# Output projection of a decode step: the last row group of wo cut into four pieces, its last row in two halves

## The chip, the cores and the metric

One core of one Trainium2 chip runs the whole kernel. The metric is device time in microseconds (us), the median of several executions. Engines are named as in the profile: PE is TensorE (PEld its weight loads), DVE is VectorE, ACT is ScalarE, POOL is GpSimd, SP is SyncE, whose queue issues all transfers here.

## What is computed

A decode step for two batch rows of width 640: cached attention with 32 heads over 4096 positions, a SiLU feed-forward, and a sigmoid gate that mixes the two.

```python
q = (x @ wq).reshape(B, 1, 32, 128)                    # x: (2, 1, 640)
p = softmax(einsum("bhqd,bhkd->bhqk", q, k_cache) * 128 ** -0.5)
o = einsum("bhqk,bhkd->bhqd", p, v_cache)              # caches: (2, 32, 4096, 128) f32
a = o.reshape(B, 1, 4096) @ wo                         # wo: (4096, 640)
b = silu(x @ w1) @ w2                                  # w1: (640, 1728)
g = sigmoid((x * gate_w).sum(-1, keepdims=True))
out = g * a + (1 - g) * b                              # (2, 1, 640)
```

All is float32. The change touches only `o @ wo`, its sum with the feed-forward's part, and the way out to memory.

## The kernel before

The kernel streams 298 MB from memory once. Sixteen items (8 groups of four heads, times 2 batch rows) each load a slab of keys and one of values, 8 MB each; POOL and DVE form the scores, ACT the exponentials, PE the weighted values. Three slabs of the on-chip memory ("v", "b", "a") are refilled in turn; slabs "v" and "b" take wo at the end, when the keys and values that lay in them are used up.

All transfers go through the SP queue in the order of the text. wo is 4096 x 640, seen as 32 "rows": one row is 128 partitions x 640 columns, 320 KB. Eight rows make a group (PR = 8), four groups make wo (NP = 4). `load_wo` (L284 to L298) issues groups 0 and 1 as one transfer, group 2 as two halves, and group 3, into slab "b", as three pieces: rows 0 to 4 (FIRST = 5), rows 5 and 6, and row 7. Each piece has its own semaphore.

PE multiplies wo by the gated attention output `oP` (each row is a contraction over 128 partitions; `oP` is the stationary operand, wo streams). Two forms are used. `in_halves` (L547) handles a row of 640 columns as two halves of 320 columns on two strips of 32 PSUM partitions, into the PSUM bank `early` (ps_acc), and does so for groups 0 to 2; the feed-forward's output was added into the same bank at the start of the kernel. `in_quarters` (L580) handles a row as four quarters of 160 columns on four strips, into the bank `acc` (ps_0), for the eight rows of group 3. Between the two `merge` (L567) brings `early` over into `acc`: ACT copies 128 x 320 from PSUM to on-chip memory (`partial`), and four matmuls with the 0/1 matrix `join` add the right strips together and set `acc`. Each matmul call of float32 stands as two MATMUL records in the trace. At the end DVE copies `acc` (128 x 160) into `ot` (L891), and SP sends eight rows of 160 floats to the output (L892).

`Flow.op` records each operation with the names that it reads and writes. A wait is made for the last writer of a name that is read; for PSUM names there is one more rule (L45, L46): an operation that reads a PSUM bank also waits for every other engine's operation that read the bank since it was last written. `once` and `spans` (L914) put stretches of an engine's program into a loop that runs once; the numbers there count operations.

Of the kernel before, what the change touches and what calls it, by code (L numbers as in the profile page):

```python
# [5 lines left out]
ALU = mybir.AluOpType  # L6
# [152 lines left out]
def gated_decode(nc, x, kc, vc, wq, wo, w1, w2, gate, out):  # L159
    P = 128  # L160
# [17 lines left out]
    G = 4  # L178
    W = D // G
    W2 = D // 2  # L180
    NP = HQ // 2
    PR = 2 * Q
    FIRST = 5
    LEAD = HB // 2
    PACED = (NP - 2) * PR
    items = [(hq, b) for hq in range(HQ) for b in range(B)]
# [7 lines left out]
    def sb(name, shape, align=32):  # L194
        return nc.alloc_sbuf_tensor(name, shape, F32, align_bytes=align)[tuple([slice(None)] * len(shape))]
# [9 lines left out]
    def part(n, *ks):  # L205
        return [f"{n}.{k}" for k in (ks or range(8))]
# [18 lines left out]
    he = sb("he", [P, FR, B])  # L225
    seq = sb("seq", [P, 2 * FR, HB])
    join = sb("join", [P, 2, HB + 1])
    turned = sb("turned", [P, FR * 32])
    mask = sb("mask", [P, B])
    spaced = sb("spaced", [P, FR, 32])  # L230
# [13 lines left out]

    ps_q, ps_o, ps_v, ps_acc, ps_t, ps_m, ps_0, ps_1 = (bank(f"ps{i}") for i in range(8))
    oT = ps_m[:64, 256:512].rearrange("p (n r) -> p n r", r=32)
    early, acc = ps_acc[:, :W2], ps_0[:, :W]

    h_q, h_e, h_v, h_o = (f.sem(n) for n in ("next_q", "weights", "values", "rows"))

# [4 lines left out]
    PD = PR * D  # L255


    partial = slab["v"][:, (NP - 1) * PD :][:, :W2]
    ot = slab["v"][:, (NP - 1) * PD + W2 :][:, :W]

    def kslab(i):
        return "a" if i % 2 == 0 else "b"
# [21 lines left out]
    def load_wo(g):  # L284

        n, at = ("v", g * PD) if g < NP - 1 else ("b", 0)
        if g == 0:
            src = wo[: 2 * PR * P, :].rearrange("(g p n) d -> p g (n d)", g=2, n=PR)
            to = slab["v"][:, : 2 * PD].rearrange("p (g c) -> p g c", g=2)
            f.dma("SP", to, src, writes=part("v", 0, 1), after=v_users)  # L290
            return
        if g == 1:
            return
        src = wo[g * PR * P : (g + 1) * PR * P, :].rearrange("(p n) d -> p (n d)", n=PR)
        cuts = (0, PD // 2, PD) if g < NP - 1 else (0, FIRST * D, PD - D, PD)
        after = f.users(part(n)) if g == NP - 1 else v_users
        for k, (c0, c1) in enumerate(zip(cuts, cuts[1:])):
            f.dma("SP", slab[n][:, at + c0 : at + c1], src[:, c0:c1], writes=part(n, g % (NP - 1) + k), after=after)  # L298
# [25 lines left out]
    f.op("POOL", lambda: G_.memset(pz, 0.0), writes=["pz"])  # L324
    f.op("POOL", lambda: G_.memset(seq, 0.0), writes=["seq"])

    out_rows = out.rearrange("b s (n d) -> (s n) b d", n=G)
    f.dma("SP", out_rows, oP[0:P:HB, :W], reads=["oP"], writes=["out"])

    f.op("DVE", lambda: V.memset(ones, 1.0), writes=["ones"])  # L330
    f.op(
# [79 lines left out]
            )  # L411

    H_AT = FH * HD
    X_AT = H_AT + B * F
# [127 lines left out]
    def heads(g):  # L544
        return [f"oP{g}{u}{b}" for u in range(2) for b in range(B)]

    def in_halves(g):  # L547

        for k in range(PR):
            s_ = g * PR + k  # L550

            def fn(k=k, s_=s_):
                to = 64 * (s_ % 2) if s_ < PACED else 0
                for n in range(2):
                    at = 32 * s_ + LEAD // 2 * n
                    last = T_.matmul(  # L556
                        early[to + 32 * n : to + 32 * n + 32, :],
                        oP[:, at : at + 32],
                        slab["v"][:, s_ * D + n * W2 : s_ * D + (n + 1) * W2],
                        start=(s_ == 0),  # L560
                        stop=(s_ in (PACED - 1, PACED + PR - 1)),
                    )
                return last

            f.op("PE", fn, reads=part("v", g + (g == NP - 2 and k >= PR // 2)) + heads(g), writes=["ps_acc"])

    def merge():  # L567
        f.op("ACT", lambda: S_.copy(partial, early), reads=["ps_acc"], writes=["partial"])

        def fn():  # L570
            for n in range(G):
                e, c = divmod(n * W, W2)
                last = T_.matmul(
                    acc[32 * n : 32 * n + HB + 1, :], join[:, e, :], partial[:, c : c + W], start=True, stop=False
                )
            return last

        f.op("PE", fn, reads=["partial", "join"], writes=["ps_0"])

    def in_quarters(g):  # L580
        for k in range(PR):
            at = LEAD + 32 * (g * PR + k)

            def fn(k=k, at=at):
                for n in range(G):
                    last = T_.matmul(  # L586
                        acc[32 * n : 32 * n + HB + 1, :],
                        oP[:, at : at + HB + 1],
                        slab["b"][:, k * D + n * W : k * D + (n + 1) * W],
                        start=False,  # L590
                        stop=(k == PR - 1),
                    )
                return last

            f.op("PE", fn, reads=part("b", (k >= FIRST) + (k == PR - 1)) + heads(g), writes=["ps_0"])

    ffn_out("v")

# [254 lines left out]
    for i in range(N + 1):  # L853
# [30 lines left out]
        if i + 1 < N:  # L884
            query(i + 1, by=[ops["relay", i]], loop=i)
            copy_q(i + 1)
    for g_ in range(NP - 1):
        in_halves(g_)
    merge()
    in_quarters(NP - 1)  # L890
    f.op("DVE", lambda: V.tensor_copy(ot, acc), reads=["ps_0"], writes=["ot"])  # L891
    f.dma("SP", out_rows, ot[0:P:HB, :], reads=["ot"], writes=["out"], signal=s_out)  # L892


    def land():
# [15 lines left out]
    f.plan()  # L911
    for e in ("SP", "POOL"):
        f.run(e)
    spans = {"ACT": (14, 34), "DVE": (100, 220), "PE": (len(f.ops["PE"]) - NP * PR - 1, len(f.ops["PE"]))}  # L914
    for e, (a, b) in spans.items():
        ops, at = f.ops[e], 0
        while at < len(ops):
# [35 lines left out]
```

## Time and profile before

| | us |
|---|---|
| median of 3 runs | 695.7 (695.59 to 695.74) |
| span of the profiled execution, first to last instruction | 694.2 |
| time outside that span (median less span) | 1.5 |
| transfer queue's share of 16 engines' span | 99.4% |
| last matmul of wo to the end of the span | about 2.1 |

The profile is of one execution. Its page has the span, the busy time of each engine, the transfer queues, the chain of work that ended last and the costliest groups of instructions. The trace behind it answers further questions: the chain in order of time, the timeline of a stretch, the groups by shape, the waits, and busy time and the granted PE clock by stretch. A row of the timeline gives start, length, engine, line, operation, operands and count of a merged run of instructions, and in brackets the idle time of that engine before it with what ended it. Ends of matmuls are modelled. In rows by shape, "busy, mean ns" gives the total in us and the mean of one in ns.

### The profile page before, as it was taken

What the parts mean: (1) busy time and instruction counts of PE and PEld (TensorE: products, weight loads), DVE (VectorE), ACT (ScalarE), POOL (GpSimd) and SP (SyncE); (2) the same over time, 40 slices, a digit from 0 to 9 for tenths busy, and PEclk for the clock granted to TensorE, in tenths of its full rate; (3) what the DMA queues carried; (4) which work ended last, traced back from release to release, by engine and by line L of the source; (5) the groups of instructions that cost most, each with busy time, mean ns of one, the idle gap of its engine ahead of it and who ended that gap; (6) DMA issues with size and microseconds to landing.
All of it is one profiled execution on the core that took longest, in us unless ns stands there. A gap on an engine that the chain in (4) does not pass through costs nothing. (4 is left out here: it accounts for less than half of the span.)

```text
span 694.2 us, 3593 instructions
## 1 busy us (share of the span) xinstructions
PE 211.4 (30%) x1440; PEld 72.5 (10%) x1440; DVE 507.5 (73%) x269; ACT 40.0 (6%) x152; POOL 265.6 (38%) x26
## 2 busy tenths in 40 slices
PE   0074032151331405060412306060503315050657
PEld 0032010010110101020100101010100101010113
DVE  3810958898989596886959596986959595977811
ACT  0001010101010101010010101010000101010000
POOL 1000808191726090815335180906244270907100
PEclk9998556565565757575665757575655757575689
DMA  9999999999999999999999999999999999999997
GB/s 383 430 446 450 430 427 424 423 457 438 427 430 423 430 461 427 434 423 423 438 457 427 430 423 427 464 430 430 423 423 461 434 430 427 423 438 457 427 408 326
DMA packets 6209, 298.33 MB, mean 430 GB/s; under 512 B 672, under 2 KB 700, under 8 KB 956
## 3 DMA queue, kind: packets, MB, share of 16 engines
q1 hardware_dynamic: 6204, 298.27, 99.4%
q8 instruction: 2, 0.03, 0.0%
q14 instruction: 3, 0.02, 0.0%
HBM read 298.26 MB, written 0.01 MB: 430 GB/s over the span
## 5 line engine op out<-in xcount | busy, mean ns | idle before, releaser
L670 POOL TENSOR_TENSOR slabs<-slabs,qsb 128x7680 f32<-128x7680 f32 x16 | 262.3, 16396 | 378.7 <-DMA slabs<-in_A_k_cache_dram 347.8
L686 DVE TENSOR_REDUCE s<-slabs 128x68 f32<-128x8704 f32 (+1 forms) x32 | 276.3, 8676 | 0.0
L766 PE MATMUL ps<-slabs,pz 128*32 128x512 f32 x1024 | 146.2, 735 | 345.2 <-PEq L145 338.2
L676 DVE TENSOR_TENSOR slabs<-slabs,ps 128x8704 f32<-128x8704 f32 x16 | 147.5, 9218 | 108.5 <-DMA slabs<-in_A_k_cache_dram 108.4
L766 PEld LDWEIGHTS ps<-slabs,pz 128*32 128x32 f32 x1024 | 39.5, 132 | 438.6 <-issue 431.6
L715 ACT ACTIVATE pz<-s,nb 32x128 f32<-32x128 f32 x64 | 25.4, 398 | 556.5 <-PE ps L766 363.2
L804 PE MATMUL ps<-osb,pick 128*128 128x512 f32 x32 | 20.4, 724 | 58.9 <-PEq L145 58.0
L818 DVE TENSOR_REDUCE row<-ps 64x128 f32<-64x512 f32 x16 | 10.9, 682 | 23.3 <-PE ps L804 23.3
L788 DVE SCALAR_TENSOR_TENSOR osb<-ps,rg,own 128x512 f32<-128x512 f32 x16 | 12.0, 748 | 21.4 <-PE ps L766 21.2
L618 PE MATMUL ps<-qall,spread 128*128 (+1 forms) x32 | 7.4, 319 | 35.3 <-PEq L145 34.5
L446 DVE SCALAR_TENSOR_TENSOR slabs<-slabs 128x1728 f32<-128x1728 f32 x8 | 16.1, 2019 | 0.3
L458 PE MATMUL ps<-slabs,xz_col 128*32 128x432 f32 x16 | 3.1, 928 | 33.2 <-DVE slabs L446 33.2
L804 PEld LDWEIGHTS ps<-osb,pick 128*128 128x128 f32 x32 | 5.4, 211 | 73.0 <-issue 71.2
L715 ACT ACTIVATION_READ_ACCUMULATOR pz<-s,nb 32x1 f32 x64 | 11.8, 184 | 0.0
L618 PEld LDWEIGHTS ps<-qall,spread 128*128 128x128 f32 x32 | 6.9, 224 | 44.9 <-issue 43.2
L533 PE MATMUL ps<-slabs,seq 128*32 128x320 f32 x54 | 10.3, 545 | 3.7 <-DVE seq L512 3.7
L825 DVE STREAM_TRANSPOSE ps<-row 64x256 f32<-64x256 f32 x16 | 10.3, 642 | 0.6
L608 PE MATMUL ps<-slabs,xz_col 128*32 128x512 f32 x80 | 9.8, 593 | 0.0
L891 DVE COPY slabs<-ps 128x160 f32<-128x160 f32 x1 | 0.3, 325 | 12.2 <-PE ps L586 12.2
L556 PE MATMUL ps<-slabs,oP_xs 128*32 128x320 f32 x96 | 8.8, 433 | 1.4 <-DMA slabs<-in_A_wo_dram 1.4
L740 PE MATMUL ps<-rs,fold 128*128 128x1 f32 x32 | 6.1, 260 | 2.3 <-PEq L145 2.1
L740 PEld LDWEIGHTS ps<-rs,fold 128*128 128x128 f32 x32 | 5.7, 222 | 5.0 <-issue 3.5
(63 smaller groups left out, 71.9 us busy)
## 6 DMA issues: line engine op xcount, KB each, us to landing
slabs<-in_A_wq_dram SPq DMA_DIRECT2D x1, 10240.0 KB, 44.5
slabs<-in_B_w_dram SPq DMA_DIRECT2D x2, 4320.0 KB, 17.0
slabs<-in_A_wo_dram SPq DMA_DIRECT2D x1, 5120.0 KB, 21.5
slabs<-in_A_wo_dram SPq DMA_DIRECT2D x2, 1280.0 KB, 25.4
slabs<-in_A_wo_dram SPq DMA_DIRECT2D x1, 1600.0 KB, 30.1
slabs<-in_A_wo_dram SPq DMA_DIRECT2D x1, 640.0 KB, 31.1
slabs<-in_A_wo_dram SPq DMA_DIRECT2D x1, 320.0 KB, 31.4
slabs<-in_A_k_cache_dram SPq DMA_DIRECT2D x16, 47.8
```

Of the source, the lines that this page charges most:

```text
L446: lambda b=b, j=j, at=at: V.scalar_tensor_tensor(hsum[:, b, :], w1t[:, j, :], at, hsum[:, b, :], op0=ALU.mult, op1=ALU.add)
L533: last = T_.matmul(early[to : to + 32, :], seq[:, k : k + 2, :].rearrange("p k z -> p (k z)"), slab[n][:, k * HD : (k + 1) * HD], start=(k ...
L618: return T_.matmul(ps_q[:, :DH], spread, qall.rearrange("p h b d -> p (h b) d")[:, i, :], start=True, stop=True,)
L670: lambda: G_.tensor_mul(k[:, CV:, :], k[:, CV:, :], qsb[:, None, :].to_broadcast([P, C - CV, DH])),
L676: lambda: V.tensor_mul(k[:, :CV, :], k[:, :CV, :], ps_q[:, None, :DH].to_broadcast([P, CV, DH])),
L686: lambda c0=c0, c1=c1: V.reduce_sum(Ss[i % 2][:, c0:c1], k[:, c0:c1, :], axis=AX.X),
L715: last = S_.activation(pz[lo:hi, :, 4 * q : 4 * q + 4], s[lo:hi].rearrange("p (g c) -> p g c", c=4), AF.Exp, bias=nb[lo:hi], scale=SCALE, ...
L740: lambda *_: T_.matmul(ps_t[:, :1], fold.rearrange("p a q c -> p (a q c)"), rs, start=True, stop=True),
L766: last = T_.matmul(ps_v[32 * q : 32 * q + 32, :], pz[:, gr, :], v[:, gr, :], start=(gr < 4), stop=(gr >= NG - 4),)
L788: lambda: V.scalar_tensor_tensor(osb, ps_v.rearrange("p (c d) -> p c d", d=DH), rg, own[:, :, None].to_broadcast([P, 4, DH]), op0=ALU.mult ...
L804: lambda *_: T_.matmul(ps_o, pick, osb.rearrange("p c d -> p (c d)"), start=True, stop=True),
L818: lambda: V.reduce_sum(row, ps_o[:64].rearrange("p (c d) -> p d c", d=DH), axis=AX.X),
```

## The change

Seven things differ.

1. Group 3 of wo is loaded in four pieces instead of three: rows 0 to 3, rows 4 and 5, row 6 with the first half of row 7 (1.5 rows), and the second half of row 7 (320 columns of each partition, 160 KB).
2. Row 0 of group 3 (HALVED = 1) is multiplied by `in_halves`, into `early`, and no longer by `in_quarters`. `merge` therefore comes after it.
3. `merge` no longer copies `early` once. ACT writes `early` times `side_of[:, 0]` into one half of `partial`, DVE writes `early` times `side_of[:, 1]` into the other (128 x 320 each). One matrix, `both`, takes the place of the two of `join`.
4. A strip now holds 80 columns of each half of the output instead of 160 neighbouring ones.
5. The first half of row 7 goes as 80 columns on four strips into `acc`, and the second half as 80 columns on four strips into a bank of its own, `rest` (ps_1).
6. ACT copies `acc` to `ot`, and DVE adds `rest` to the second 80 columns of it. Both transfers to the output have 16 runs of 80 floats where they had 8 of 160.
7. Two small DVE operations at the start make `both` (17 columns) and `side_of` (2 columns).

```diff
--- before.py
+++ after.py
@@ -178,9 +178,11 @@
     G = 4
     W = D // G
     W2 = D // 2
+    W4 = W // 2
     NP = HQ // 2
     PR = 2 * Q
-    FIRST = 5
+    HALVED = 1
+    CUTS = (0, 4, 6)
     LEAD = HB // 2
     PACED = (NP - 2) * PR
     items = [(hq, b) for hq in range(HQ) for b in range(B)]
@@ -225,6 +227,8 @@
     he = sb("he", [P, FR, B])
     seq = sb("seq", [P, 2 * FR, HB])
     join = sb("join", [P, 2, HB + 1])
+    both = sb("both", [P, HB + 1])
+    side_of = sb("side_of", [P, 2])
     turned = sb("turned", [P, FR * 32])
     mask = sb("mask", [P, B])
     spaced = sb("spaced", [P, FR, 32])
@@ -244,7 +248,7 @@
     ps_q, ps_o, ps_v, ps_acc, ps_t, ps_m, ps_0, ps_1 = (bank(f"ps{i}") for i in range(8))
     oT = ps_m[:64, 256:512].rearrange("p (n r) -> p n r", r=32)
-    early, acc = ps_acc[:, :W2], ps_0[:, :W]
+    early, acc, rest = ps_acc[:, :W2], ps_0[:, :W], ps_1[:, : W // 2]
     h_q, h_e, h_v, h_o = (f.sem(n) for n in ("next_q", "weights", "values", "rows"))
@@ -255,8 +259,8 @@
     PD = PR * D
-    partial = slab["v"][:, (NP - 1) * PD :][:, :W2]
-    ot = slab["v"][:, (NP - 1) * PD + W2 :][:, :W]
+    partial = slab["v"][:, (NP - 1) * PD :][:, :D].rearrange("p (e c) -> p e c", e=2)
+    ot = slab["v"][:, (NP - 1) * PD + D :][:, :W]
     def kslab(i):
         return "a" if i % 2 == 0 else "b"
@@ -292,7 +296,7 @@
         if g == 1:
             return
         src = wo[g * PR * P : (g + 1) * PR * P, :].rearrange("(p n) d -> p (n d)", n=PR)
-        cuts = (0, PD // 2, PD) if g < NP - 1 else (0, FIRST * D, PD - D, PD)
+        cuts = (0, PD // 2, PD) if g < NP - 1 else (*(k * D for k in CUTS), PD - W2, PD)
         after = f.users(part(n)) if g == NP - 1 else v_users
         for k, (c0, c1) in enumerate(zip(cuts, cuts[1:])):
             f.dma("SP", slab[n][:, at + c0 : at + c1], src[:, c0:c1], writes=part(n, g % (NP - 1) + k), after=after)
@@ -324,8 +328,12 @@
     f.op("POOL", lambda: G_.memset(pz, 0.0), writes=["pz"])
     f.op("POOL", lambda: G_.memset(seq, 0.0), writes=["seq"])
-    out_rows = out.rearrange("b s (n d) -> (s n) b d", n=G)
-    f.dma("SP", out_rows, oP[0:P:HB, :W], reads=["oP"], writes=["out"])
+    out_rows = out.rearrange("b s (e n d) -> (s n) b e d", e=2, n=G)
+    def two_ends(t):
+        return t[0:P:HB, :W].rearrange("p (e d) -> p e d", e=2)
+    f.dma("SP", out_rows, two_ends(oP), reads=["oP"], writes=["out"])
     f.op("DVE", lambda: V.memset(ones, 1.0), writes=["ones"])
     f.op(
@@ -411,6 +419,9 @@
             )
+    f.op("DVE", lambda: V.tensor_add(both, join[:, 0, :], join[:, 1, :]), reads=["join"], writes=["both"])
+    f.op("DVE", lambda: V.reduce_sum(side_of, join, axis=AX.X), reads=["join"], writes=["side_of"])
     H_AT = FH * HD
     X_AT = H_AT + B * F
@@ -546,53 +557,70 @@
     def in_halves(g):
-        for k in range(PR):
+        last_row = NP * PR - PR + HALVED - 1
+        for k in range(PR if g < NP - 1 else HALVED):
             s_ = g * PR + k
-            def fn(k=k, s_=s_):
+            w = slab["v"][:, s_ * D : (s_ + 1) * D] if g < NP - 1 else slab["b"][:, k * D : (k + 1) * D]
+            which = part("v", g + (g == NP - 2 and k >= PR // 2)) if g < NP - 1 else part("b", 0)
+            def fn(s_=s_, w=w):
                 to = 64 * (s_ % 2) if s_ < PACED else 0
                 for n in range(2):
                     at = 32 * s_ + LEAD // 2 * n
                     last = T_.matmul(
                         early[to + 32 * n : to + 32 * n + 32, :],
                         oP[:, at : at + 32],
-                        slab["v"][:, s_ * D + n * W2 : s_ * D + (n + 1) * W2],
+                        w[:, n * W2 : (n + 1) * W2],
                         start=(s_ == 0),
-                        stop=(s_ in (PACED - 1, PACED + PR - 1)),
+                        stop=(s_ in (PACED - 1, last_row)),
                     )
                 return last
-            f.op("PE", fn, reads=part("v", g + (g == NP - 2 and k >= PR // 2)) + heads(g), writes=["ps_acc"])
+            f.op("PE", fn, reads=which + heads(g), writes=["ps_acc"])
     def merge():
-        f.op("ACT", lambda: S_.copy(partial, early), reads=["ps_acc"], writes=["partial"])
+        f.op("ACT", lambda: S_.mul(partial[:, 0, :], early, side_of[:, 0:1]), reads=["ps_acc", "side_of"], writes=["partial0"])
+        f.op(
+            "DVE",
+            lambda: V.tensor_scalar(partial[:, 1, :], early, side_of[:, 1:2], None, op0=ALU.mult),
+            reads=["ps_acc", "side_of"],
+            writes=["partial1"],
+        )
         def fn():
             for n in range(G):
-                e, c = divmod(n * W, W2)
                 last = T_.matmul(
-                    acc[32 * n : 32 * n + HB + 1, :], join[:, e, :], partial[:, c : c + W], start=True, stop=False
+                    acc[32 * n : 32 * n + HB + 1, :],
+                    both,
+                    partial[:, :, n * W4 : (n + 1) * W4],
+                    start=True,
+                    stop=False,
                 )
             return last
-        f.op("PE", fn, reads=["partial", "join"], writes=["ps_0"])
+        f.op("PE", fn, reads=["partial0", "partial1", "both"], writes=["ps_0"])
     def in_quarters(g):
-        for k in range(PR):
-            at = LEAD + 32 * (g * PR + k)
-            def fn(k=k, at=at):
+        to = acc.rearrange("p (e c) -> p e c", e=2)
+        for k in range(HALVED, PR + 1):
+            r, cols = min(k, PR - 1), slice(k == PR, 1 + (k != PR - 1))
+            at = LEAD + 32 * (g * PR + r)
+            w = slab["b"][:, r * D : (r + 1) * D].rearrange("p (e n c) -> p n e c", e=2, n=G)
+            def fn(k=k, at=at, w=w, cols=cols):
                 for n in range(G):
+                    strip = slice(32 * n, 32 * n + HB + 1)
                     last = T_.matmul(
-                        acc[32 * n : 32 * n + HB + 1, :],
+                        rest[strip, :] if k == PR else to[strip, cols, :],
                         oP[:, at : at + HB + 1],
-                        slab["b"][:, k * D + n * W : k * D + (n + 1) * W],
-                        start=False,
-                        stop=(k == PR - 1),
+                        w[:, n, cols, :],
+                        start=(k == PR),
+                        stop=(k >= PR - 1),
                     )
                 return last
-            f.op("PE", fn, reads=part("b", (k >= FIRST) + (k == PR - 1)) + heads(g), writes=["ps_0"])
+            piece = sum(k >= c for c in CUTS[1:]) + (k == PR)
+            f.op("PE", fn, reads=part("b", piece) + heads(g), writes=["ps_1" if k == PR else "ps_0"])
     ffn_out("v")
@@ -884,12 +912,13 @@
         if i + 1 < N:
             query(i + 1, by=[ops["relay", i]], loop=i)
             copy_q(i + 1)
-    for g_ in range(NP - 1):
+    for g_ in range(NP):
         in_halves(g_)
     merge()
     in_quarters(NP - 1)
-    f.op("DVE", lambda: V.tensor_copy(ot, acc), reads=["ps_0"], writes=["ot"])
-    f.dma("SP", out_rows, ot[0:P:HB, :], reads=["ot"], writes=["out"], signal=s_out)
+    f.op("ACT", lambda: S_.copy(ot, acc), reads=["ps_0"], writes=["ot"])
+    f.op("DVE", lambda: V.tensor_add(ot[:, W4:], ot[:, W4:], rest), reads=["ot", "ps_1"], writes=["ot"])
+    f.dma("SP", out_rows, two_ends(ot), reads=["ot"], writes=["out"], signal=s_out)
     def land():
@@ -911,7 +940,7 @@
     f.plan()
     for e in ("SP", "POOL"):
         f.run(e)
-    spans = {"ACT": (14, 34), "DVE": (100, 220), "PE": (len(f.ops["PE"]) - NP * PR - 1, len(f.ops["PE"]))}
+    spans = {"ACT": (14, 34), "DVE": (102, 222), "PE": (len(f.ops["PE"]) - NP * PR - 2, len(f.ops["PE"]))}
     for e, (a, b) in spans.items():
         ops, at = f.ops[e], 0
         while at < len(ops):
```

## Rows read from the trace of the kernel before

**Rows 1.** The page, queues: packets, MB, share of 16 engines' span.

```profile
q1 hardware_dynamic: 6204, 298.27, 99.4%
```

**Rows 2.** The chain that ended last, in order of time: start, us, what.

```profile
659.21 30.07 DMA slabs<-in_A_wo_dram
689.28 0.14 issue
689.42 2.19 PE ps L586 x56
...
691.61 0.51 PE ps L586 x8
...
692.15 0.33 DVE slabs L891
```

**Rows 3.** Timeline from 687.45 us to the end: start, us, instruction, idle before.

```profile
687.22 0.98 PE L556 MATMUL ps<-slabs,oP_xs 128*32 128x320 f32 x6
...
688.25 0.43 ACT L568 COPY slabs<-ps 128x320 f32<-128x320 f32 x1 [28.38 <-PE ps L556]
...
688.73 0.47 PE L573 MATMUL ps<-slabs,join 128*17 128x160 f32 x8 [0.53 <-ACT slabs L568]
...
690.87 0.41 PEld L586 LDWEIGHTS ps<-slabs,oP_xs 128*17 128x17 f32 x16 [0.23 <-DMA slabs<-in_A_wo_dram]
...
692.50 0.58 SPq L69 DMA_DIRECT2D out_dram<-slabs  x1
```

**Rows 4.** Loads of group 3: size of each, us from issue to landing.

```profile
slabs<-in_A_wo_dram SPq DMA_DIRECT2D x1, 1600.0 KB, 30.1
slabs<-in_A_wo_dram SPq DMA_DIRECT2D x1, 640.0 KB, 31.1
slabs<-in_A_wo_dram SPq DMA_DIRECT2D x1, 320.0 KB, 31.4
```

**Rows 5.** What SP waited for, and how long issues took (ns, min/median/max).

```profile
SPq L69 <- DVE slabs L891: 31.8, 1, 31.8
...
L69 SPq DMA_DIRECT2D slabs<-in_A_wo_dram x6: 378/432/468, 657.8 to 660.2; - x6
...
L69 SPq DMA_DIRECT2D oP_xs<-in_A_x_dram x1: 730/730/730, 1.9 to 1.9; - x1
```

**Rows 6.** Timeline of the setup, DVE: its first instruction after the constants.

```profile
13.75 0.46 DVE L420 STREAM_TRANSPOSE slabs<-oP_xs 128x160 f32<-128x160 f32 x1 [7.72 <-DMA oP_xs<-in_gate_w_dram]
```

**Rows 7.** Groups by shape: matmuls of 320 and of 160 columns.

```profile
L556 PE MATMUL ps<-slabs,oP_xs 128*32 128x320 f32 x96 | 8.8, 433 | 1.4 <-DMA slabs<-in_A_wo_dram 1.4
...
L586 PE MATMUL ps<-slabs,oP_xs 128*17 128x160 f32 x64 | 2.7, 301 | 0.2 <-DMA slabs<-in_A_wo_dram 0.2
```

**Rows 8.** Groups by shape: ACT, then DVE, operations with the new ones' kinds.

```profile
L640 ACT COPY qsb<-ps 128x128 f32<-128x128 f32 x16 | 4.3, 267 | 5.9 <-PE ps L618 5.8
L647 ACT ACTIVATE qall<-ps,mask 128x512 f32<-128x512 f32 x4 | 2.4, 689 | 20.3 <-PE ps L608 20.3
...
L788 DVE SCALAR_TENSOR_TENSOR osb<-ps,rg,own 128x512 f32<-128x512 f32 x16 | 12.0, 748 | 21.4 <-PE ps L766 21.2
...
L831 DVE TENSOR_SCALAR oE<-ps,side 64x8 f32<-64x8 f32 x16 | 3.5, 218 | 0.6
...
L505 DVE TENSOR_TENSOR he<-he,gc 128x28 f32<-128x28 f32 x1 | 0.2, 189 | 0.0
```

**Rows 9.** Timeline of 689.0 to 690.8 us: the five rows of piece 0.

```profile
689.42 1.55 PE L586 MATMUL ps<-slabs,oP_xs 128*17 128x160 f32 x40 [0.23 <-DMA slabs<-in_A_wo_dram]
```

**Rows 10.** By stretch: us, PE busy (count), granted clock, DMA share, GB/s.

```profile
660.40:663.66 3.26, 0.00 (x0) 1.00 1.25 543
663.67:667.07 3.40, 0.00 (x0) 0.50 0.63 271
```

**Rows 11.** Timeline: PE's start on wo, and weight loads at the 0.50 clock.

```profile
679.39 0.48 PE L556 MATMUL ps<-slabs,oP_xs 128*32 128x320 f32 x4 [1.40 <-DMA slabs<-in_A_wo_dram]
...
649.69 0.23 PEld L766 LDWEIGHTS ps<-slabs,pz 128*32 128x32 f32 x4 [0.63 <-issue]
```

## The prediction

> **What bounds the kernel now.** I read the page first. The transfer queue is busy for 99.4% of the span [rows 1], so up to the last load the time is that of moving 298 MB, and a change to the arithmetic can matter only where the loads end. Next the chain of waits: it comes down the loads of wo to 689.28 us, then runs through PE (seven rows of group 3 in 2.19 us, with a pause in them, then row 7), DVE's copy and SP [rows 2]. The pieces land 30.1, 31.1 and 31.4 us after their issues [rows 4], which follow each other by some 0.45 (0.43 each [rows 5], and a hand): 689.28, about 690.8 and about 691.55. PE stands still 0.23 us until 690.87 for the second [rows 3], and takes row 7 at 691.61 [rows 2], as the third has landed. So PE is ahead of the loads and the last landing sets the end. What stands behind that landing is short: PE 0.51, DVE 0.33 [rows 2], SP's issue at 692.50 [rows 3], and 1.70 until the span ends at 694.2.
>
> The important reading is how far PE is ahead. ACT's copy of `early` (0.43) and the `join` matmuls (0.47, from 688.73) end at 689.20, just before piece 0 lands [rows 2, 3]: `merge` is hidden in the wait for piece 0. With all data there, PE would be ready for row 7 at about 690.9 against the 691.61 at which it starts; it has some 0.7 us in hand.
>
> **The loads.** Two rows land between 689.28 and 690.8, and the third 0.75 behind them, so a row takes about 0.77. Piece 0, a row shorter, lands at 688.51; rows 4 and 5 at about 690.05; row 6 and half of row 7 at about 691.2. The last half lands where row 7 did, at 691.55, plus what a fourth piece of 128 short runs costs: taken as 0.05, between 0 (the bytes are the same) and 0.37 (half a row at the speed of the whole row). This is covered, as will be seen, by 1.0 us. The fourth issue costs SP 0.43, inside the 31.8 us in which it waits for the result [rows 5]. The two operations that make `both` and `side_of` lie in DVE's idle 7.72 us ahead of 13.75 [rows 6]. The first transfer to the output, now with 16 runs, is 5 KB among 298 MB. All three: nothing.
>
> **Row 0 and `merge`.** Here the change moves work. Row 0 goes into `early`, so everything in `merge` now stands behind piece 0, where before it stood ahead of it. PE starts row 0 at 688.51 + 0.14 (the step behind piece 0 in [rows 2]; at least 0.04, about the step behind the other pieces) = 688.65. A row in halves is two pairs of 320-column matmuls. Three pairs take 0.98 [rows 3]; one matmul lasts 0.43 [rows 7], so a pair follows a pair by 0.27, and two pairs end after 0.71: 689.36.
>
> Then two copies. Both read `early`, in one bank, and by L45 and L46 the second waits for the first: DVE starts only when ACT has finished. ACT's multiply by a column: 128 x 512 took 0.689; plain copies took 0.267 (128 columns) [rows 8] and 0.43 (320) [rows 3], 0.83 ns a column, so 0.689 less 192 columns is 0.53; no less than the plain copy's 0.43, no more than 0.69. DVE's multiply by a column of 320: 0.218 for 8 columns and 0.748 for 512 (two tensor inputs, the nearest row from above) [rows 8], 1.05 ns a column: 0.55. A hand from PE to ACT and from ACT to PE takes 0.05 each [rows 3]; I take 0.05 for each of the three hands here. So 689.36 + 0.05 + 0.53 + 0.05 + 0.55 + 0.05 = 690.59 for the `join` matmuls, where they ran at 688.73. Queued behind them on PE are rows 1 to 7, all of them.
>
> [...]
>
> **Rows 1 to 7.** Five rows take 1.55 [rows 9] as ten steps of half a row each, the last one lasting as long as the `join` matmuls' second step: (1.55 − 0.47) / 8 = 0.135 a step, 0.27 a row. `join` is one row: row 1 starts at 690.59 + 0.27 = 690.86, six rows later, at 692.48, the first half of row 7. All its data landed at 691.2 or before, so PE waits for no load any more, and the last landing (691.6) comes 1.0 us ahead of its use. Half a row is two steps of 80 columns: 0.07 each if a step goes by columns, 0.135 if it has a floor at that; I take 0.07. A matmul lasts 433 ns at 320 and 301 at 160 columns [rows 7], so 235 at 80; with the strips' stagger of 0.02 the first half is done 0.07 + 0.02 + 0.235 = 0.33 after its start: 692.81. The second half, on PE behind it, is done by 692.95, while ACT copies.
>
> **The end.** ACT copies 160 columns: 0.267 + 32 x 0.83 ns = 0.29, from 692.86 to 693.15. DVE's addition waits for it (0.05) and takes 0.189 (28 columns [rows 8]) + 52 x 1.05 ns = 0.24: 693.44. SP issues 0.02 later, at 693.46, where it did at 692.50 [rows 3]: **0.96 later**. The output leaves as 16 runs of 320 bytes where there were 8 of 640. No row has that; the issue may cost nothing more, or 0.15 more (0.73, the longest small issue [rows 5], against 0.58 [rows 3]). I take 0.05, nearer to the output's own row. [...]
>
> **Sum.** The profiled span of 694.2 becomes 695.2. The median of the runs, 695.7, lies 1.5 above the span, which I keep: **696.7**. With every bound low (0.10 off the first step, 0.10 off ACT's multiply, 0.08 off the addition, 0.05 off the output) it is 696.4; with the high ones (0.16 on ACT's multiply, 0.13 on two steps of 80 columns, 0.10 on the output) 697.1.
>
> **Rivals.**
> The two copies run side by side: for it speaks that they write different halves of `partial`, against it L45. Then ACT's 0.53 and a hand drop out and `join` starts at 690.0: 696.1, or 695.8 with the low bounds.
>
> The last landing still sets the end, and the smaller remainder gains: landing 691.60, half a row 0.06 + 0.33 to 691.99, DVE 0.07 + 0.24, SP at 692.32, 0.18 earlier; with the output's 0.05, 695.6. For that `join` would have to start by about 689.45, but row 0 is only done at 689.36. Almost excluded.
>
> PE's clock falls, on the slower side. PE now stands idle for 1.2 us between row 0 and `join`, after 0.5 before row 0. [...] At the low level four 512-column matmuls take 0.86 [rows 11], twice what 0.135 for 160 columns gives. From `join` to the end of row 7 PE has 2.2 us of work on the path; a fall at `join` adds 2.2 (698.9), one halfway 1.1 (697.8). It decides for slower by 0.2% as soon as more than 0.4 us of that work is done at the low level.
>
> That the change does not do what it says: the trace would show the second half of row 7 with the first, or ACT's copy behind both. It would add about 0.15, within the bounds.
>
> **How the numbers follow.** A measurement of this kernel can tell 0.2%, 1.4 us, from no change. Chances: the forecast 0.79, of which 0.01 lies above 697.1; copies side by side 0.05; the landing 0.01; the clock 0.10; something the trace does not show, 0.05 (0.01 faster, 0.01 same, 0.03 slower). Same: 0.78 + 0.05 + 0.01 + 0.01 = 0.85; slower: 0.01 + 0.10 + 0.03 = 0.14; faster 0.01. The range covers the forecast's bounds and the copies side by side with their low bounds: 695.9; above, the high bounds with a little of the clock's case: 697.4. It leaves out most of the clock's case and the unseen.
>
> **What would show it.** In the profile after: row 0 of group 3 at about 688.65; ACT's multiply, then DVE's after its end; `join` at 690.6; rows 1 to 7 without a pause for a load; SP's issue near 693.5, clock 1.00 to there. DVE's multiply starting with ACT's, a pause of PE for the last piece, or a lower clock behind 690 would prove me wrong, each in the way given above.

## The result

| | median, us | span (median of runs) | time outside the span |
|---|---|---|---|
| kernel before (10 runs; spans from the 33 runs beside the first experiments) | 695.72 | 694.3 | 1.36 |
| kernel after (10 runs) | 697.39 (696.95 to 697.53) | 695.4 | 1.81 |

The medians differ by 1.67 us, 0.24%. The ratio on record is 1.0019 with a 95% interval of 1.0011 to 1.0028, which reaches to both sides of the 0.2% that a measurement can tell. Forecast were 696.7 and a range of 695.9 to 697.4; the time lies 0.01 below the range's upper end. About 1.1 us of the loss lies in the span and about 0.45 outside it, where the forecast had 1.0 and nothing. "Outside" is the median, over the runs, of a run's time less its own span.

The timeline of the changed kernel's end (start, us, engine, line, operation, operands, count, idle before it), against [rows 3] and [rows 9]:

```profile
688.86 0.73 PE L570 MATMUL ps<-slabs,oP_xs 128*32 128x320 f32 x4 [0.45 <-DMA slabs<-in_A_wo_dram]
689.63 0.53 ACT L582 ACTIVATE slabs<-ps,side_of 128x320 f32<-128x320 f32 x1 [30.55 <-PE ps L570]
690.19 0.55 DVE L585 TENSOR_SCALAR slabs<-ps,side_of 128x320 f32<-128x320 f32 x1 [9.36 <-ACT slabs L582]
...
690.80 0.47 PE L592 MATMUL ps<-slabs,both 128*17 128x160 f32 x8 [1.20 <-DVE slabs L585]
690.95 2.02 PEld L613 LDWEIGHTS ps<-slabs,oP_xs 128*17 128x17 f32 x64
691.08 2.09 PE L613 MATMUL ps<-slabs,oP_xs 128*17 128x160 f32 x64
693.10 0.29 ACT L919 COPY slabs<-ps 128x160 f32<-128x160 f32 x1 [2.94 <-PE ps L613]
693.42 0.24 DVE L920 TENSOR_TENSOR slabs<-slabs,ps 128x80 f32<-128x80 f32 x1 [2.68 <-ACT slabs L919]
693.69 0.58 SPq L69 DMA_DIRECT2D out_dram<-slabs  x1
```

Row 0 waits 0.45 for piece 0. Then PE waits 1.20 for the two copies, and from `join` on it runs without a pause: the weight loads of rows 1 to 7 are one row of the timeline with no wait in it, where in [rows 3] one of them waits 0.23 for a piece. The chain that ended last has the same (start, us, what). Like the one in [rows 2] it comes off the loads at piece 0; but there PE's 56 records behind it took 2.19, with a wait inside, and here 56 take 1.81 in steps of 0.136, with none, and the two copies and `join` stand ahead of them:

```profile
658.43 30.30 DMA slabs<-in_A_wo_dram
688.73 0.14 issue
688.86 0.75 PE ps L570 x4
...
689.63 0.54 ACT slabs L582
...
690.19 0.56 DVE slabs L585
...
690.80 0.47 PE ps L592 x8
691.27 1.81 PE ps L613 x56
...
693.10 0.30 ACT slabs L919
...
693.42 0.24 DVE slabs L920
```

By stretch (us, PE busy and count, granted clock, DMA share, GB/s), PE's last run of the changed kernel stands at a granted clock of 1.00, as does the stretch before it with PE's pause:

```profile
690.80:693.17 2.37, 2.37 (x72) 1.00 0.03 12
688.86:690.79 1.93, 0.73 (x4) 1.00 0.71 280
```

Outside the span something else moved. The page's queue table, asked for a stretch, has transfers of the kind "instruction", which I read as program loads. Behind 693.4 us the kernel before has only its output on the queues (first fence below). The kernel after has a load of 8 KB on queue 14 that begins between 694.0 and 694.1, and another that begins between 696.1 and 696.2, after its span has ended at 695.4 (second and third). Columns: packets, MB, share of 16 engines.

```profile
q1 hardware_dynamic: 12, 0.01, 0.4%
```

```profile
q14 instruction: 1, 0.01, 20.2%
```

```profile
q14 instruction: 1, 0.01, 30.8%
```

The kernel before has the same two loads, but at 690.27 and 692.65, before its span ends. Its last work on ACT was released at 688.25 [rows 3]; in the kernel after that is at 693.10, the new copy of `acc`. That gave the theory for the experiments: queue 14 brings ACT's program, the two loads follow ACT's last work, and the end of the execution waits for them. The runs below bear out that the loads and the end follow ACT's last release; that the end waits for a load stays argued, and for the first of the two at most.

### The profile page after: what moved, and what is told of

It reads as the page before. It is cut to its first block, busy times and chain, and to the rows that moved or that the text cites. A ratio compares the mean times of both kernels' runs of the same rounds, so it can differ in the third digit from the quotient of the medians.

```text
span 695.4 us, 3607 instructions
## 1 busy us (share of the span) xinstructions
PE 209.9 (30%) x1444; PEld 72.4 (10%) x1444; DVE 508.3 (73%) x272; ACT 40.4 (6%) x153; POOL 266.2 (38%) x26
```

## The experiments

Medians in us, spans and time outside as above; the kernel before, run beside them, had 695.7 to 695.9.

| run | row 0 | copies in `merge` | last copy by | median | span | outside |
|---|---|---|---|---|---|---|
| before | acc | 1 | DVE | 695.76 | 694.3 | 1.36 |
| before, ACT copies last | acc | 1 | ACT | 696.68 | 694.5 | 2.02 |
| before, idle ACT copy at the end | acc | 1 | DVE | 697.05 | 695.2 | 1.97 |
| before, longer idle ACT copy | acc | 1 | DVE | 697.03 | 695.0 | 1.88 |
| before, idle DVE copy at the end | acc | 1 | DVE | 696.07 | 694.7 | 1.34 |
| before, row 7 lands in halves | acc | 1 | DVE | 695.90 | 694.6 | 1.33 |
| after | early | 2 | ACT | 697.39 | 695.4 | 1.81 |
| after, DVE copies last | early | 2 | DVE | 696.95 | 695.5 | 1.38 |
| after, row 0 in acc | acc | 2 | ACT | 696.74 | 694.6 | 2.06 |
| after, row 0 in acc, DVE copies last | acc | 2 | DVE | 696.59 | 694.9 | 1.71 |
| after, one copy, DVE copies last | early | 1 | DVE | 697.29 | 694.7 | 2.59 |
| the same, one small DVE operation more | early | 1 | DVE | 697.37 | 694.8 | 2.59 |
| after, row 0 in acc, one copy, DVE last | acc | 1 | DVE | 696.11 | 694.7 | 1.39 |
| halves into acc, one DVE copy | acc | 1 | DVE | 696.03 | 694.5 | 1.49 |

### Who works last

The kernel before with ACT in DVE's place:

```diff
-    f.op("DVE", lambda: V.tensor_copy(ot, acc), reads=["ps_0"], writes=["ot"])
+    f.op("ACT", lambda: S_.copy(ot, acc), reads=["ps_0"], writes=["ot"])
```

> The kernel before, with one change: ACT instead of DVE copies acc into ot at the end. Theory A (the change's time outside the span grew because ACT now works last: its program's 8 KB loads on queue 14 came at 690.27 and 692.65 in the profile before, after ACT's last operation at 688.68, and at 694.02 and 696.13 in the profile after, after its last at 693.39): the span loses some 0.05 (0.29 us for ACT's copy against 0.33, a shorter hand), yet the median rises by 0.3 to 0.5, to about 696.1; the two loads follow ACT's end. Rival B (the time outside grew through the 16-run output, the fourth load piece or run-to-run spread): no such rise, 695.6 to 695.7.

Measured: 696.68, 0.92 more than the kernel before, with a profiled span of 694.2 as before. More than the 0.3 to 0.5 expected, and mostly outside the span (2.02 for 1.36; the median span is 0.2 longer). In its timeline SP issues 0.06 earlier than in [rows 3]:

```profile
692.12 0.29 ACT L891 COPY slabs<-ps 128x160 f32<-128x160 f32 x1 [3.47 <-PE ps L586]
692.44 0.58 SPq L69 DMA_DIRECT2D out_dram<-slabs  x1
```

Its two loads on queue 14 begin at 693.06 and 695.18. Then the opposite cut, work on ACT that nobody waits for until SP's wait for the output:

```diff
+    f.op("ACT", lambda: S_.copy(slab["b"][:, :W], ot), reads=["ot"], writes=["spare"])
     f.dma("SP", out_rows, ot[0:P:HB, :], reads=["ot"], writes=["out"], signal=s_out)
...
-    f.op("SP", land).signal = "sent"
+    f.op("SP", land, reads=["spare"]).signal = "sent"
```

> The kernel before, with a copy of ot by ACT behind DVE's last copy, whose result nobody uses; SP issues the output without waiting for it, and only its wait for the output comes behind it. Theory A: the span stays 694.2 within 0.1, the median rises by 0.3 to 0.5 to about 696.1, since ACT's program ends 4 us later. Rival B: both stay, 695.7.

Measured: 697.05, 1.29 more, for a copy off the path. The time outside rose by 0.61, somewhat more than expected; the span rose too, by 0.9, which was not expected. In the profile the output lands 2.08 us after its issue, where it took 1.68 in the kernel before. The load on queue 14 lies from 693.80 to 694.27, and the last two of the output's eight packets start at 694.27 and 694.30, the others at 694.16 or before. That agrees with the load standing ahead of them on one DMA engine; it was not tried by itself.

```profile
692.86 0.58 SPq L69 DMA_DIRECT2D out_dram<-slabs  x1
692.87 0.33 ACT L892 COPY slabs<-slabs 128x160 f32<-128x160 f32 x1 [3.84 <-DVE slabs L891]
```

The same idle copy on DVE (`V.tensor_copy` for `S_.copy`):

> The kernel before with a copy of ot by DVE behind its last copy, whose result nobody uses; as in the run with an idle ACT copy (697.05), SP issues the output without waiting for it. Theory (only ACT has program code to load at its end, the two loads of 8 KB that follow its last operation): no cost, 695.7 to 695.8. Rival (any engine that ends late costs): about 697.

Measured: 696.07, 0.23 above the runs beside it, in the span (694.7 against 694.5), with an unchanged 1.34 outside.

```profile
692.81 0.24 DVE L892 COPY slabs<-slabs 128x160 f32<-128x160 f32 x1
```

The intervals of the two ratios, 1.0007 to 1.0025 for ACT and 0.9994 to 1.0013 for DVE, overlap. The times outside do not: 1.84 to 2.11 in all eleven runs with the copy on ACT, 1.31 to 1.50 in all eleven with it on DVE. So it is not any engine that ends late; the same copy in the same place moved the median by 1.29 on ACT and by 0.23 on DVE.

A longer idle copy on ACT, 960 columns:

```diff
-    f.op("ACT", lambda: S_.copy(slab["b"][:, :W], ot), reads=["ot"], writes=["spare"])
+    f.op("ACT", lambda: S_.copy(slab["b"][:, :960], slab["b"][:, 1600:2560]), reads=["ot", "ps_0"], writes=["spare"])
```

> The kernel before with a longer idle ACT operation at its end: 960 columns, about 0.99 us, where the run with 160 columns had 0.33 and a median of 697.05. Theory (the end of the program waits for ACT, whose two 8 KB loads come one after the other behind its last operation, so the time follows ACT's end one for one): ACT ends 0.66 later, the median is 697.7; the first load now falls behind the output's packets, so the span goes back to 694.3 and the time outside it to 3.4. Rival (a fixed price for ACT being last, paid once): 697.0, or less with the span back.

Measured: 697.03, no more than with the short copy; the rival's number. The theory in the form "time follows the end of ACT's last work" falls. The trace says why: ACT works until 693.85, but the load begins between 693.75 and 693.85 (queue table of that stretch), 0.94 after the copy's start, as it did with the short copy.

```profile
692.86 0.99 ACT L892 COPY slabs<-slabs 128x960 f32<-128x960 f32 x1 [3.82 <-DVE slabs L891]
```

```profile
q14 instruction: 1, 0.01, 23.0%
```

So the loads follow the moment at which ACT's last operation is released, not its end. From that moment to the first load it is 0.94 (ACT in DVE's place), 0.93 and 0.94 (idle copies), 0.92 (the kernel after) and 0.93 (after, row 0 in acc); the second load is 2.12 behind the first in each; and the time of each of the five profiled executions is its release, counted from the span's start, plus 4.0 to 4.3. Against the rival's fixed price speaks that between ACT in DVE's place and the idle copy the release differs by about 0.36 (DVE's copy and a hand), and the medians by 0.37; by themselves these two numbers could also be the output's later landing. Where ACT is released by 689.7, while wo is still coming in, the first load begins 0.95 to 2.02 behind the release, both loads are over by 693.3, ahead of the output's landing, and 1.3 to 1.4 is left outside the span in most kernels.

What decides between the two stands in the kept traces, which hold every update of a semaphore (a counter by which engines wait for one another), those past the span's end too. Behind each kernel's work semaphore 2 is written nine times in a row, then the other semaphores are written in blocks, then semaphore 2 nine times again. In seven of the nine profiles without a late ACT the ninth write comes 0.30 to 0.31 behind the span's end (the other two are treated below, under "One copy in `merge`"). In the five with ACT released late it comes 0.59 to 0.83 behind it, but 2.91 to 2.95 behind ACT's release in every one. So the end goes by ACT's release, and not by the end of the span plus a fixed price. The second load begins 0.12 after the ninth write, so these writes do not wait for it. That the first one is what holds them up is argued from the order and was not tried by itself. What the nine writes are for, no run here shows.

Last, the changed kernel with DVE for ACT:

```diff
-    f.op("ACT", lambda: S_.copy(ot, acc), reads=["ps_0"], writes=["ot"])
+    f.op("DVE", lambda: V.tensor_copy(ot, acc), reads=["ps_0"], writes=["ot"])
```

> The changed kernel, with DVE instead of ACT for the copy of acc; DVE's addition behind it stays. Theory A: the span stays within 0.1 (DVE's copy takes 0.33 for ACT's 0.29), the time outside it falls to that of the kernel before, and the median falls from 697.4 to about 697.0. Rival B: no change in the time outside, 697.4.

Measured: 696.95, 0.44 less than the kernel after, all of it outside (1.38 for 1.81). The span is 695.5 for 695.4; both moves are those expected.

```profile
693.14 0.33 DVE L919 COPY slabs<-ps 128x160 f32<-128x160 f32 x1 [2.36 <-PE ps L613]
693.50 0.24 DVE L920 TENSOR_TENSOR slabs<-slabs,ps 128x80 f32<-128x80 f32 x1
693.76 0.58 SPq L69 DMA_DIRECT2D out_dram<-slabs  x1
```

### `merge` behind piece 0

```diff
-    HALVED = 1
+    HALVED = 0
```

> The changed kernel with HALVED = 0: row 0 of group 3 goes into acc as in the kernel before, so merge stands ahead of piece 0 again; all else as changed. Theory (the longer path is merge moved behind piece 0): the join matmuls start by about 689.5 instead of 690.8, row 7 ends about 692.1, SP issues near 692.6 to 692.8 against 693.69; the median falls by about 1.0 to 696.4. Rival (the copies and the last row's pieces themselves are the cost, wherever merge stands): the median stays above 697.

Measured: 696.74, with a span 0.8 shorter (694.6). `join` starts at 689.79, not at 689.5, and SP issues at 692.95, not at 692.6 to 692.8:

```profile
688.62 0.53 ACT L582 ACTIVATE slabs<-ps,side_of 128x320 f32<-128x320 f32 x1 [28.16 <-PE ps L570]
689.19 0.55 DVE L585 TENSOR_SCALAR slabs<-ps,side_of 128x320 f32<-128x320 f32 x1 [8.69 <-ACT slabs L582]
...
689.79 0.47 PE L592 MATMUL ps<-slabs,both 128*17 128x160 f32 x8 [1.21 <-DVE slabs L585]
690.07 2.36 PE L613 MATMUL ps<-slabs,oP_xs 128*17 128x160 f32 x72
692.36 0.29 ACT L919 COPY slabs<-ps 128x160 f32<-128x160 f32 x1 [3.21 <-PE ps L613]
...
692.95 0.58 SPq L69 DMA_DIRECT2D out_dram<-slabs  x1
```

The copies start a microsecond earlier than in the kernel after (688.62 for 689.63), ahead of piece 0, which here lands at 688.9. With the second copy, `join` still comes later than the loads need; PE runs through once more. And ACT is still released late (692.36): 2.06 outside. With DVE's copy at the end beside it:

> The changed kernel with DVE's copy at the end and HALVED = 0: beside the run with DVE's copy alone (696.95) it takes row 0 out of early, beside the run with ACT at the end and HALVED = 0 (696.74) it takes ACT away from the end. Theory (merge behind piece 0 costs about 0.7 on the path, ACT's end the rest): the span is 694.7 as there, the time outside falls to 1.35, the median is 696.1. Rival (ACT's end is not what lengthened the run with HALVED = 0): 696.7.

Measured: 696.59, nearer to the rival's 696.7 than to the 696.1 of the theory. It is 0.36 below the run with row 0 in `early` and DVE at the end, where about 0.85 was expected, and only 0.15 below the run with ACT at the end. The span gives 0.6 (694.9 for 695.5), but the time outside is 1.71 and not 1.35. ACT was released at 688.44 and its loads were over by 692.4, so ACT is not what makes this 1.71, and no program load stands in the trace behind it. Nor is the end longer in the profiled execution (1.72 outside): semaphore 2 is written for the last time 1.46 behind the span's end, as in the runs with row 7 in halves, which have 1.34 outside in theirs. What makes the difference is open.

### One copy in `merge`

ACT copies `early` once and plainly, and the two matrices of `join` do the rest; DVE keeps the copy at the end, as in the run that had 696.95:

```diff
-        f.op("ACT", lambda: S_.mul(partial[:, 0, :], early, side_of[:, 0:1]), reads=["ps_acc", "side_of"], writes=["partial0"])
-        f.op(
-            "DVE",
-            lambda: V.tensor_scalar(partial[:, 1, :], early, side_of[:, 1:2], None, op0=ALU.mult),
-            reads=["ps_acc", "side_of"],
-            writes=["partial1"],
-        )
+        f.op("ACT", lambda: S_.copy(flat, early), reads=["ps_acc"], writes=["partial0"])
...
+            for e in range(2):
+                for n in range(G):
+                    last = T_.matmul(
+                        acc[32 * n : 32 * n + HB + 1, e * W4 : (e + 1) * W4],
+                        join[:, e, :], flat[:, n * W4 : (n + 1) * W4], start=(e == 0), stop=False)
```

> The changed kernel with DVE's copy of acc at the end (as in the run before that had 696.95) and with one copy in merge: ACT copies early once, plainly, and eight matmul calls of 80 columns with the two matrices of join set acc; DVE's multiply is gone. Row 0 still goes into early. Theory (the two copies one after the other are on the path): the join matmuls start at about 690.1 instead of 690.8, the median falls by 0.65 to about 696.3. Rival (PE behind them sets the end anyway): 696.9.

Measured: 697.29, more and not less, although the path did as expected. `join` starts at 690.03, SP issues at 692.96, 0.80 before the kernel with two copies and DVE at the end, and the span is 0.8 shorter:

```profile
689.55 0.42 ACT L583 COPY slabs<-ps 128x320 f32<-128x320 f32 x1 [30.24 <-PE ps L570]
...
690.03 0.47 PE L588 MATMUL ps<-slabs,join 128*17 128x80 f32 x16 [0.52 <-ACT slabs L583]
...
692.96 0.59 SPq L69 DMA_DIRECT2D out_dram<-slabs  x1
```

The gain is lost outside the span: 2.59, in all eleven runs 2.2 or more. Here a load of 16 KB on queue 8 begins between 692.95 and 693.05 (queue table of that stretch), as DVE's last operation ends at 692.93, and is done at 694.13:

```profile
q8 instruction: 1, 0.02, 70.7%
```

I took this for chance: a load of DVE's program that happens to fall there. One more DVE operation in the setup should then move it (the stretch of DVE's program that goes into a loop moves along by one):

```diff
+    f.op("DVE", lambda: V.memset(both, 0.0), writes=["both"])
     f.op("DVE", lambda: V.tensor_add(both, join[:, 0, :], join[:, 1, :]), reads=["join"], writes=["both"])
```

> The run with one copy in merge, row 0 in early and DVE's copy at the end (median 697.29, span 694.7, 2.59 outside it) with one more small DVE operation in the setup, where DVE has 7 us to spare. There a 16 KB program load on queue 8 came at 693.00, right behind DVE's last operation at 692.93. Theory (such a load, by where DVE's program happens to be cut, made the 2.6, and the form of merge has nothing to do with it): the load moves away from the end, the time outside falls to about 1.4 and the median to 696.1 to 696.3, 0.7 below the run with two copies (696.95). Rival (the form of the kernel itself makes the 2.6): 697.3 again.

Measured: 697.37, again 2.59 outside, and again a load on queue 8 near the end, from 693.47 to 694.42, though now 0.69 behind the end of DVE's last operation and not at it. So one operation more does not take it away, and the guess falls.

The semaphore updates point to PE and not to DVE. The first of the nine writes of semaphore 2 comes 0.20 to 0.36 behind the end of PE's last matmul in the twelve other profiles. In these two it comes 3.35 and 3.79 behind it (at 695.76 and 696.05), and 1.63 behind the end of the load on queue 8 in both. That agrees with a load of PE's program which PE needs for its end. It is argued from the order of these times; no run changed PE's program by itself for this. What does move the load is a difference on PE: with row 0 in `acc` and the same operations on DVE, ACT, POOL and SP, it comes at 684.68, while PE is busy with wo, and the time outside is 1.39:

> The same, and row 0 in acc (HALVED = 0): what is left of the change is the four pieces, the last half row in a bank of its own with DVE's addition, and the 16-run output. Theory (all of the loss was merge behind piece 0, its second copy, and ACT as the last engine but one): join starts at 688.7 as in the kernel before, the last landing sets the end again, SP issues at about 692.35, the median is 695.6, 0.1 to 0.2 below the kernel before. Rival (the pieces, the addition or the 16 runs cost by themselves): 696.0 or more.

Measured: 696.11 against 695.84 beside it, not the 695.6 expected. `join` is at 688.90 (688.7 expected), and the loads set the end again: row 6 and the two halves of row 7 wait for the third piece. But the path behind that piece is longer than I had counted, since row 6 lies in it too, and DVE's copy can only follow all of it:

```profile
688.90 0.47 PE L588 MATMUL ps<-slabs,join 128*17 128x80 f32 x16 [0.53 <-ACT slabs L583]
689.19 1.96 PE L609 MATMUL ps<-slabs,oP_xs 128*17 128x160 f32 x48
691.53 0.74 PE L609 MATMUL ps<-slabs,oP_xs 128*17 128x160 f32 x24 [0.39 <-DMA slabs<-in_A_wo_dram]
692.21 0.32 DVE L915 COPY slabs<-ps 128x160 f32<-128x160 f32 x1 [11.84 <-PE ps L609]
692.56 0.24 DVE L916 TENSOR_TENSOR slabs<-slabs,ps 128x80 f32<-128x80 f32 x1
```

From the third piece (691.49) to the end of the addition (692.80) it is 1.31; the fourth piece, 0.39 later, was never waited for. So the cut of the pieces, too, takes back what the shorter last half gives.

### The fourth piece, and a version with the gain alone

```diff
-        cuts = (0, PD // 2, PD) if g < NP - 1 else (0, FIRST * D, PD - D, PD)
+        cuts = (0, PD // 2, PD) if g < NP - 1 else (0, FIRST * D, PD - D, PD - W2, PD)
```

PE's row 7 waits for both of the last two.

> The kernel before with the load of row 7 cut into two transfers of half a row each; PE still takes row 7 when both have landed. It prices the fourth piece alone. Theory (0.05 for 128 more, short runs): the last landing 0.05 later, median 695.8. Rival (the later last landings in the profiles with four pieces, 691.8 to 692.0 against 691.5 to 691.9, are the pieces' doing): 0.25 later, 696.0.

Measured: 695.90 against 695.84, 0.06 more, near the 0.05 of the forecast. The interval of the ratio, 0.9993 to 1.0012, does not exclude the rival's 0.25.

The last run takes only what should help: pieces of 5, 2, 0.5 and 0.5 rows, row 7 as two halves of 80 columns on four strips, both into `acc`, one plain copy in `merge`, DVE's one copy at the end.

> A version meant to be the best of both: the kernel before (row 0 in acc, one plain copy of early by ACT, one copy of acc by DVE), with row 7 cut into two halves of 80 columns on four strips, both into acc, pieces of 5, 2, 0.5 and 0.5 rows, and the 16-run output. Theory: behind the last landing it needs 0.04 + 0.33 + 0.07 + 0.33 = 0.77 where the kernel before needs 0.91, less 0.05 for the fourth piece: the median is 0.1 below the kernel before, 695.7, and not to be told from it. Rival (pieces and 16 runs cost more than they give): 696.0 or more.

Measured: 696.03 against 695.71: not to be told from the kernel before, and if anything later. None of the versions beats the kernel before. In the last run's profile a load of 16 KB on queue 8 begins at 693.76, 0.57 behind DVE's last operation, and that execution has only 1.34 outside; semaphore 2 had been written for the first time at 693.15, ahead of that load. So this load near the end did not cost by itself.

## Why the prediction held, point by point

**That the loads would no longer set the end** held: PE ran from `join` to the end without a pause, and the last landing (691.8) came 1.04 before its use (the second half of row 7 starts at 692.85), where 1.0 was worked out.

**Row 0 and `merge`.** Step by step, forecast and measured: ACT's multiply 0.53 and 0.528; DVE's 0.55 and 0.550, begun 0.03 after ACT's end, so one after the other as L45 and L46 have it; row 0 0.71 and 0.73. From piece 0's landing to SP's issue the sum was 4.95 (688.51 to 693.46); the profile has 4.96 (688.73 to 693.69). What was off is the landing itself, 0.22 late in this execution; profiles of the four-piece kernels have it from 688.5 to 688.9.

**The end.** ACT's copy 0.29 and 0.292, DVE's addition 0.24 and 0.239; a step of 80 columns 0.07 and 0.069, so there is no floor at 0.135. The output's 16 runs cost nothing that shows, where 0.05 was put in: issue 0.58 as before, and 1.69 from issue to landing for 1.68.

**What was wrong** is one sentence: "the median of the runs, 695.7, lies 1.5 above the span, which I keep". Run by run the kernel before has 1.36, and it is no constant of the program. The change moves the last copy from DVE to ACT, and I priced that as a copy and its hands. With DVE back in that place the time outside is 1.38 and the median 696.95, 0.25 from the forecast. The 0.44 between goes with ACT's late release. It could have been seen: the queue table of the page counts the program loads, and the trace has two on queue 14 close to the end, with ACT idle since 688.68. That the time still fell into the range, by 0.01, is luck: its upper end was drawn there for a little of the clock's case, and the clock did not fall there.

**The rivals.** The clock stayed at 1.00 through PE's pause of 1.2; its fall to 0.50 in [rows 10] came behind 3.26 us without PE work, and whether and after how long a pause brings it down, no run here tried. The copies did not run side by side, and the last landing did not set the end. Something that the sum had no term for did come, ACT's late release, but too small to make the kernel slower by a clear margin, which is what the 0.03 stood for; and the trace of before did show the program loads, in a row that I had not read for this. The range's lower end, 695.9, leaves out the 695.8 that the sum gives for copies side by side with low bounds.

**How much each part costs.** The spans say it, since the medians are blurred by the time outside. Row 0 in `early` with two copies: 695.4 and 695.5. Row 0 in `acc` with two copies: 694.6 and 694.9. Row 0 in `early` with one copy: 694.7 and 694.8. Both away: 694.7. So the two do not add up: each of them alone fits into the time that PE has in hand, and only together do they cost 0.6 to 0.8. The prediction had them as two terms of one sum, which was right for the kernel as changed, but either could have stayed. What is left to the kernel before (694.3 to 694.5) no run takes apart; the cut of the pieces, the addition behind the copy and the 16-run output are what still differs.

**Still open**: what makes the 1.71 outside with row 0 in `acc`, two copies and DVE last, whether the load on queue 8 is PE's, as the semaphore updates suggest, and why one row on PE moves it by 8 us.

## What to carry to other kernels

Here `merge` had been hidden in the wait for piece 0; behind that load and with a second copy in it, `join` started at 690.80 instead of 688.73 [rows 3] and SP issued at 693.69 instead of 692.50. Look for what stands ahead of the piece you cut, not only at the piece, and count how much slack it uses up together with the other parts. Ask of an operation moved to another engine whether that engine now works last, and look in the queue table for program loads near the end: ACT in DVE's place for one copy of 0.3 us cost 0.92 in the kernel before, 0.44 in the changed one and 0.15 with row 0 in `acc`, mostly outside the span. Read the span and the time outside it apart, run by run, before a median is put down to the path.

## What was not expected of the hardware

- Work on ACT at the very end of the program cost more than its length: an idle copy of 0.33 us on ACT made the kernel 1.29 slower, the same copy on DVE (0.24 us) 0.23. In the five profiles with ACT released late, two loads of 8 KB follow its last release by 0.92 to 0.94 and by 2.12 more, the ninth write of semaphore 2 follows it by 2.91 to 2.95, and the execution's time is that release plus 4.0 to 4.3, whether the operation takes 0.3 or 1.0 us.
- A program load of 16 KB on queue 8 behind PE's last matmul and ahead of the first write of semaphore 2 goes with 2.59 us outside the span in two kernels, against 1.36; one that began after that write, at 693.76, went with 1.34.
- Four strips of 80 columns step at 0.069 us, half of the 0.136 for 160 columns: no floor down to this size.
